# Batch 0's scores and head of softmax in two halves of the tokens, with the mask of the second w_in piece between the halves

**Chip, cores, metric.** One core of one Trainium2 chip. The metric is the device time of one execution in microseconds; the profiled span is about 2 us shorter than that time (750.4 against 752.25 in the profiled run of before). Most comparisons below are of one to four microseconds in 753, so each is backed twice: by timed runs in rounds with the kernel before on the same chip, and by the moment at which one landmark, the first up-projection matmul, starts in the profile.

## The reference

Cross-attention of tokens x (8 batches, 8 heads, 512 tokens, 64 wide) with a small state (32 rows), in both directions, then a two-layer feed-forward with a quick GELU on all 4352 rows.

```python
scores = scale * np.matmul(x, state.transpose(0, 1, 3, 2))
a = softmax(scores);   xread = np.matmul(a, state)      # softmax over the 32 state rows
scores2 = scale * np.matmul(state, x.transpose(0, 1, 3, 2))
a2 = softmax(scores2); sread = np.matmul(a2, x)         # softmax over the 512 tokens
x = concat(xread, sread) reshaped to (B*544, 512)
h = x @ w_in
g = h * (1.0 / (1.0 + np.exp(-1.702 * h)))
out = g @ w_out
```

The weights arrive as float64, so the kernel converts them itself: each of the 16 pieces of w_in is masked (VectorE), turned into a power of two by two Relus (ScalarE), and assembled in four further VectorE instructions ("rounding" below).

## The kernel before

The parts that the change touches, with cuts marked "...".

```python
    def keep_warm(n):                       # fillers: nothing reads the result
        ps = psH.tile([P, FC], FP32, tag="h", name="warm")
        for _ in range(n):
            nc.tensor.matmul(ps, zeros[:, :P], zeros, start=True, stop=True)
    ...
    def round_a(i):
        ...
        nc.vector.tensor_scalar(sc, hi, 0x7FF00000, None, ALU.bitwise_and)          # the mask
        ...
        nc.scalar.activation(out=sc.bitcast(FP32), in_=sc, func=AF.Relu, bias=edge[0], scale=-8.0)
        nc.scalar.activation(out=sc, in_=sc.bitcast(FP32), func=AF.Relu, bias=edge[1], scale=-1.0)
    ...
    def att_xT_arriving(b, warm):
        A[b]["xT"] = apool.tile([P, NPR, S], FP32, tag="xT", name=f"xT_{b}")
        for c in range(SCH):                                                        # 4 chunks of 128 tokens
            keep_warm(warm)
            ps = att_ps([P, NPR, P], f"xT_{b}_{c}")
            for j in range(NPR):
                nc.tensor.transpose(ps[:, j], x_heads(b, c, j), ident)
            (nc.scalar.copy if c % 2 else nc.vector.tensor_copy)(A[b]["xT"][:, :, P * c : P * (c + 1)], ps)
    ...
    load_weights(1); load_state(0); load_x(0); load_weights(NPR); load_state(1); load_x(1); ...   # one per line
    keep_warm(11)
    round_to(1, 0)               # mask, Relus and rounding of piece 0
    att_state(0)
    att_xT_arriving(0, 2)
    att_scores(0)                # 8 matmuls of 512 columns
    powers_to(2)                 # mask and Relus of piece 1
    att_blocks(0)                # VectorE: two transposes of 512 columns
    att_x_exp(0)                 # VectorE: maximum, subtraction; ScalarE: exponential
    round_to(2, 1)
    att_x_norm(0)
    keep_warm(24)
    att_state(1)
    ...                          # batch 1's transposes and scores
    keep_warm(24)
    powers_to(4)
    round_to(NPR, 2)             # pieces 2 and 3
    att_M(0, 0)                  # M(0,0): w_in's first 512 columns times batch 0's state
    att_blocks(1)
    att_x_exp(1)
    up_x(0, 0)                   # first up-projection matmul: the landmark
    ...
```

## Time and profile before

| | before |
|---|---|
| median of three runs, and their spread | 752.65 us, 752.60 to 754.64 |
| profiled span | 750.4 us |
| TensorE busy | 731.6 us, 98% |
| M(0,0) starts | 29.05 us |
| first up-projection matmul starts | 30.89 us |

The page's clock row, one digit for each fortieth of the span (18.8 us), shows the TensorE clock that was granted; a 9 is full speed or nearly. The trace's record of the clock begins with its first change, at 6.06 us; ahead of it the view shows 1.00, while the eleven fillers of the start took 4.88 us, 0.43 each, twice their later 0.22.

```profile
PEclk9999999999999999999999999999999999999999
```

In a view by stretches, a line holds the stretch in us, its length, the busy time of TensorE, its weight loads, VectorE, ScalarE and GpSimd, the granted clock, and the transfers. In the kernel before two stretches are:

```profile
12.00:18.00 6.00, 6.00 (x43) 2.65 (x28) 5.39 (x9) 2.99 (x4) 0.00 (x0) 1.00 0.99 254
18.00:24.00 6.00, 5.49 (x42) 2.86 (x41) 5.83 (x10) 3.71 (x8) 0.00 (x0) 1.00 1.01 322
```

VectorE is busy for 5.4 and 5.8 of 6 us. Below, M(b,c) is the product of w_in's c-th 512 columns with batch b's state.

### The profile page before, as it was taken

The page shows a single profiled execution, that of the slowest core. Times are in us where ns is not written, and L with a number is a line of the kernel's source. Part 1 is how long each engine was busy: PE and PEld are TensorE (multiplying, and loading weights), DVE is VectorE, ACT ScalarE, POOL GpSimd, SP SyncE. Part 2 cuts the span into 40 slices and gives each one's busy share as a digit, 9 for nine tenths or more (in the row PEclk, how much of TensorE's full clock was granted, in tenths as well). Part 3 has the DMA queues.
Part 4 walks back from the last instruction along what each step waited for, and adds up shares of the span by engine and source line. Part 5 has one row for each costly group of instructions (what it writes and reads, how often), then busy time and mean ns, then how long its engine had stood idle before and what let it go on. Part 6 is the DMA issues. An engine that isn't in the chain of part 4 may idle for free.

```text
span 750.4 us, 10915 instructions
## 1 busy us (share of the span) xinstructions
PE 731.6 (98%) x4555; PEld 567.4 (76%) x4555; DVE 501.7 (67%) x947; ACT 232.1 (31%) x421; POOL 0.8 (0%) x8
## 2 busy tenths in 40 slices
PE   8989999999999999999999999999999999999996
PEld 3433444467888789878888789878887888899995
DVE  5999799615846775567747666677656774768340
ACT  4676511022324511433134322451143313300220
POOL 0000000000000000000000000000000000000000
PEclk9999999999999999999999999999999999999999
DMA  9811245010030000300040003000030001000000
GB/s 236 331 58 56 93 160 144 0 57 1 29 83 5 1 16 29 74 1 15 2 102 1 15 2 93 10 1 16 29 74 1 15 2 42 1 15 29 15 1 28
DMA packets 48768, 35.29 MB, mean 47 GB/s; under 512 B 36432, under 2 KB 44112, under 8 KB 48720
## 3 DMA queue, kind: packets, MB, share of 16 engines
q1 hardware_dynamic: 48720, 34.61, 16.1%
q8 instruction: 35, 0.57, 0.3%
q14 instruction: 13, 0.11, 0.1%
HBM read 25.69 MB, written 8.91 MB: 46 GB/s over the span
## 4 chain that ended last, share of the span: by engine, by line
PE 94%; SPq 2%; ACT 2%; DMA 1%; DVE 1%; issue 0%; DVEq 0%; ACTq 0%
PE o L645 28%; PE o L890 16%; PE o L522 9%; PE h L461 8%; PE o L479 7%; PE low L597 6%; PE upx L890 6%; PE o L597 4%; PE M L279 4%; PE xT L261 1%; SPq L138 1%; PE sr L410 1%; PE o L279 1%; PE upx_sr L890 1%; DMA out_dram<-osb_sr 1%; PE warm L122 1%
## 5 line engine op out<-in xcount | busy, mean ns | idle before, releaser
L900 DVE TENSOR_TENSOR g<-o,g 128x512 f32<-128x512 f32 (+1 forms) x140 | 88.1, 651 | 87.3 <-PE o L890 86.3
L645 PE MATMUL o<-w_out,g 128*128 128x256 f32 x576 | 130.0, 380 | 0.0
L645 PEld LDWEIGHTS o<-w_out,g 128*128 128x128 f32 x576 | 107.4, 190 | 18.1 <-issue 4.2
L897 ACT ACTIVATE g<-g 128x512 f32<-128x512 f32 (+1 forms) x84 | 49.8, 600 | 100.5 <-DVE g L900 100.5
L890 PE MATMUL o<-ta,M 128*128 128x256 f32 x192 | 49.3, 379 | 0.0
L890 PE MATMUL upx<-aT,M 128*128 128x256 f32 x192 | 49.3, 379 | 0.0
L890 PE MATMUL o<-ta,ms 128*128 128x256 f32 x192 | 48.4, 380 | 0.0
L390 ACT COPY M<-M 128x512 f32<-128x512 f32 x64 | 33.2, 596 | 42.5 <-PE M L279 42.5
L645 PE MATMUL o<-sums,g 128*128 128x256 f32 x192 | 43.8, 382 | 0.0
L522 PE MATMUL o<-w_out,g 128*128 128x256 f32 x192 | 42.9, 380 | 0.0
L645 PE MATMUL o<-sums,later 128*128 128x256 f32 x192 | 42.4, 379 | 0.0
L645 PEld LDWEIGHTS o<-sums,g 128*128 128x128 f32 x192 | 35.6, 190 | 8.6 <-issue 4.2
L522 PEld LDWEIGHTS o<-w_out,g 128*128 128x128 f32 x192 | 36.1, 190 | 6.0 <-issue 1.3
L890 PEld LDWEIGHTS o<-ta,ms 128*128 128x128 f32 x192 | 36.4, 190 | 5.2 <-DVE osb L541 0.3
L890 PEld LDWEIGHTS o<-ta,M 128*128 128x128 f32 x192 | 36.5, 190 | 5.0
L645 PEld LDWEIGHTS o<-sums,later 128*128 128x128 f32 x192 | 36.5, 190 | 5.0
L890 PEld LDWEIGHTS upx<-aT,M 128*128 128x128 f32 x192 | 36.5, 190 | 5.0
L502 DVE TENSOR_TENSOR later<-g,g 128x512 f32<-128x512 f32 (+1 forms) x32 | 20.8, 650 | 21.5 <-ACT g L464 21.5
L279 PE MATMUL M<-w_in,stT 64*32 64x512 f32 x512 | 33.2, 594 | 0.2 <-ACT eT L400 0.2
L461 PE MATMUL h<-low,M 128*128 128x512 f32 x64 | 29.8, 600 | 2.1 <-ACT M L390 2.1
L461 PE MATMUL h<-aT,M 128*128 128x512 f32 x64 | 28.7, 599 | 2.3 <-ACT M L390 2.3
L600 DVE TENSOR_TENSOR pu<-low,pu 128x128 f32<-128x128 f32 x12 | 3.5, 291 | 39.6 <-PE low L597 39.6
(172 smaller groups left out, 1136.6 us busy)
## 6 DMA issues: line engine op xcount, KB each, us to landing
later<-in_moe_w_out_dram SPq DMA_DIRECT2D x16, 512.0 KB
xn<-in_x_dram SPq DMA_DIRECT2D x28, 256.0 KB
w_out<-in_moe_w_in_dram SPq DMA_DIRECT2D x12, 512.0 KB
out_dram<-osb SPq DMA_DIRECT2D x20, 256.0 KB
out_dram<-later SPq DMA_DIRECT2D x12, 256.0 KB
later<-in_moe_w_in_dram SPq DMA_DIRECT2D x4, 512.0 KB
sums<-in_x_dram SPq DMA_DIRECT2D x4, 256.0 KB
stn<-in_state_dram SPq DMA_DIRECT2D x16, 32.0 KB
```

The lines of the kernel that those rows point to most:

```text
L122: nc.tensor.matmul(ps, zeros[:, :P], zeros, start=True, stop=True)
L279: nc.tensor.matmul(ps[g][st], A[b]["stT"][rows, st], rhs(rows, j), start=True, stop=True)
L390: nc.scalar.copy(m[:, g], ps[g])
L461: nc.tensor.matmul(hps, lhs[i], rhs[i], start=(i == 0), stop=(i == n - 1))
L479: nc.tensor.matmul(ops, G[key, f // 2][:, f % 2, P * r : P * (r + 1)], w_out[:, f], start=(f == 0), stop=(f == NF - 1))
L502: nc.vector.tensor_tensor(out=s1, in0=a21, in1=a22, op=ALU.add)
L522: nc.tensor.matmul(ps[:, r], lhs[f][:, P * r : P * (r + 1)], rhs[:, f], start=(first and r == 0 and f == 0), stop=(f == HF - 1), skip_grou ...
L597: nc.tensor.matmul(ps, lhs[f], rhs[:, f], start=(f == 0), stop=(f == QF - 1))
L645: nc.tensor.matmul(ps[:, r], lhs[f][:, P * r : P * (r + 1)], rhs[:, f], start=(r == 0 and f == 0), stop=(f == HF - 1), skip_group_check=True,)
L890: nc.tensor.matmul(ps[:, k], lhs[i][:, o : o + P], rhs[i], start=(first and k == 0 and i == 0), stop=(i == n - 1), skip_group_check=True,)
L897: nc.scalar.activation(out=dst, in_=src, func=AF.Gelu_apprx_sigmoid)
L900: nc.vector.tensor_tensor(out=dst, in0=ps, in1=x, op=ALU.add)
```

## The change

The intent: VectorE, which paces the opening, waits until all four chunks of batch 0's x have been transposed. If it begins after two of them, its work on the first half lies in time that it had spent waiting. The mask of piece 1 goes between the halves, where VectorE would wait again. As M(0,0) is expected earlier, ten fillers go.

```diff
         for c in range(SCH):
-            keep_warm(warm)
+            if c < 2:
+                keep_warm(warm)
             ps = att_ps([P, NPR, P], f"xT_{b}_{c}")
             ...
-            (nc.scalar.copy if c % 2 else nc.vector.tensor_copy)(A[b]["xT"][:, :, P * c : P * (c + 1)], ps)
+            (nc.scalar.copy if c else nc.vector.tensor_copy)(A[b]["xT"][:, :, P * c : P * (c + 1)], ps)
+            if c % 2:
+                att_half(b, c // 2)
+            if c == 1:
+                powers_to(2)
...
+    def att_half(b, i):
+        ...
+        by_state(b, ps, lambda rows, j: a["xT"][rows, j, n * i : n * (i + 1)])     # 8 matmuls of 256 columns
+        for g in range(NG):
+            nc.vector.transpose(a["e1"][:, g, w].rearrange("p i n -> p (i n)"), ps[g])
+        t, mx = a["e1"][:, :, w], a["mx"][:, :, w]
+        nc.vector.reduce_max(out=mx, in_=t, axis=AX.X)
+        nc.vector.tensor_tensor(out=t, in0=t, in1=mx.to_broadcast((P, NG, NB // 2, Ns)), op=ALU.subtract)
...
     att_xT_arriving(0, 2)
+    nc.scalar.activation(out=A[0]["e1"], in_=A[0]["e1"], func=AF.Exp, scale=scale)
     att_scores(0)
     powers_to(2)
-    att_blocks(0)
-    att_x_exp(0)
...
     att_scores(1)
-    keep_warm(24)
+    keep_warm(14)
     powers_to(4)
```

More of the change, by code (lines that the diff above doesn't have):

```diff
@@ L279, in by_state @@
                 nc.tensor.matmul(ps[g][st], A[b]["stT"][rows, st], rhs(rows, j), start=True, stop=True)
+    def att_half(b, i):
+        a = A[b]
+        if i == 0:
+            a["e1"] = apool.tile([P, NG, NB, Ns], FP32, tag="e1", name=f"e1_{b}")
+            a["mx"] = apool.tile([P, NG, NB], FP32, tag="mx", name=f"mx_{b}")
+        n, w = S // 2, slice(NB // 2 * i, NB // 2 * (i + 1))
+        ps = [v[:, :n] for v in bank_o[NG:]] if i else [psH.tile([P, n], FP32, tag="h", name=f"sh_{b}_{g}") for g in range(NG)]
+        by_state(b, ps, lambda rows, j: a["xT"][rows, j, n * i : n * (i + 1)])
[4 more added lines that the diff above has]
+        nc.vector.tensor_tensor(out=t, in0=t, in1=mx.to_broadcast((P, NG, NB // 2, Ns)), op=ALU.subtract)
     def att_scores(b):
```

## The prediction

> **What bounds the kernel now.** I read the page first. The first line of its busy times, and its chain that ended last (PE 94%), say that nearly the whole span is TensorE work, and the change removes none of that: it touches only the opening, some 30 us of 750.

> ```profile
> PE 731.6 (98%) x4555; PEld 567.4 (76%) x4555; DVE 501.7 (67%) x947; ACT 232.1 (31%) x421; POOL 0.8 (0%) x8
> ```

> So the question is when steady TensorE work starts. The chain of work over the first 60 us (start us, duration us, what) answers:

> ```profile
> 15.03 4.10 DMA sums<-in_x_dram
> ...
> 22.10 1.73 PE o L279 x16
> 23.83 5.29 PE warm L122 x24
> 29.11 1.16 PE M L279 x16
> ...
> 30.89 7.15 PE h L461 x16
> ```

> The chain runs through the arrival of batch 1's x, then batch 1's scores, then 24 filler matmuls (L122 only keeps the array busy), then M(0,0), the product of w_in with batch 0's state at 29.1. A chain through filler needs a second reading: filler is there to fill, so something else may end at the same moment. The timeline of the opening shows it (start us, duration us, engine, line, operation, in brackets idle time and releaser):

> ```profile
> 1.19 4.88 PE L122 MATMUL warm<-sums 128*128 128x512 bf16 x11 [1.19 <-DVE one L113]
> 8.46 0.59 ACT L272 COPY xT<-xT 128x512 f32<-128x512 f32 x1 [1.58 <-PE xT L271]
> 8.70 0.69 DVE L272 COPY xT<-xT 128x512 f32<-128x512 f32 x1
> 10.77 0.59 ACT L272 COPY xT<-xT 128x512 f32<-128x512 f32 x1 [1.72 <-PE xT L271]
> 11.41 1.09 PE L279 MATMUL o<-xT,stT 64*32 64x512 f32 x16 [0.67 <-ACT xT L272]
> 11.63 0.43 DVE L189 TENSOR_SCALAR low<-w_out 128x512 int32<-128x512 int32 x1 [1.14 <-DMA w_out<-in_moe_w_in_dram]
> 12.09 0.72 ACT L194 ACTIVATE low<-low,edge 128x512 f32<-128x512 int32 x1 [0.73 <-DVE low L189]
> 12.44 5.35 PE L122 MATMUL warm<-sums 128*128 128x512 bf16 x24
> 12.59 1.31 DVE L292 STREAM_TRANSPOSE e<-o 128x512 f32<-128x512 f32 x2 [0.54 <-PE o L279]
> 13.94 1.22 DVE L328 TENSOR_REDUCE mx<-e 128x32 f32<-128x1024 f32 x1
> 15.20 1.22 DVE L329 TENSOR_TENSOR e<-e,mx 128x1024 f32<-128x1024 f32 x1
> 16.34 0.42 DVE L189 TENSOR_SCALAR low<-w_out 128x512 int32<-128x512 int32 x1
> ...
> 28.12 0.69 DVE L207 SCALAR_TENSOR_TENSOR w_in<-w_in,low 128x512 f32<-128x512 f32 x1
> ...
> 29.05 1.09 PE L279 MATMUL M<-w_in,stT 64*32 64x512 f32 x16
> ```

> From 12.59 to 28.81 (28.12 + 0.69) VectorE has no wait: head of batch 0's softmax, then rounding of w_in pieces, with piece 3 last. M(0,0) needs piece 3 and starts 0.24 later. Hence **VectorE is the real bound of the opening**, and the 24 fillers are sized to end with it. The time from the end of the subtraction (15.20 + 1.22 = 16.42) to piece 3 is 12.39 us of unchanged VectorE work. After M(0,0) the chain is matmuls, evictions and short Relus, and TensorE is almost without gaps from 49 us on, so a shift of M(0,0) should reach the end whole.

> [...] ScalarE's instructions up to 31 us stand in program order. [...] 11 fillers in 4.88 us (0.43 each) at the start, against 24 in 5.35 (0.22) later[...]. [...] a reduction over 1024 elements takes 1.22 us and one over 512 (L299, later) 0.68, so two halves cost 0.14 more.

> **The change part by part.** *Removed:* two pairs of fillers in front of the third and fourth chunk of x; VectorE's copy of chunk 2 (0.69, now a ScalarE copy of 0.59); ten of the later fillers (10 x 0.22 = 2.2 us of TensorE). *Added:* two half-width score products on TensorE (the full one stays, because the second softmax reads it). Their matmuls are half as long, so about 0.5 us each in the queue and about 0.65 to the first result (1.09 less half of 0.86, the latter being the spacing of 16 such matmuls in row "PE M L279 x32", 1.72 us). On VectorE, per half: two transposes of 256 columns. With (1.22 - 0.68)/512 = 1.05 ns per column, 0.72 becomes 0.45 and the pair 0.77 us; a reduction over 512, 0.68; a subtraction over 512, about 0.69; two gaps of 0.04: 2.22 us. Two halves are 4.44 against 3.83 (12.59 to 16.42), so 0.6 more VectorE work, to be repaid by starting earlier.

> *Moved:* the mask of piece 1 (L189) with its two ScalarE Relus (L194, L195), from behind the scores to between the halves. This is the step on which I decide. My timetable:
> - VectorE copies chunk 0 to 9.39 as now. Half-scores 0 on TensorE 9.44 to 10.1. VectorE half 0 from 10.2 to 12.45. Its mask of piece 1 about 12.4 to 12.8 (the data has been there since 11.63).
> - TensorE transposes chunks 2 and 3 by about 11.1. Their copies are both on ScalarE, and in its program they stand **behind the two Relus of piece 1**, which wait for the mask, which waits for half 0. Relus from 12.85 to 14.3, copy of chunk 2 to 14.85, of chunk 3 to 15.4.
> - Half-scores 1 at 15.45, first result 16.2; VectorE, idle since 12.8 (some 3.4 us), does half 1 from 16.3 to 18.5.
> - 18.5 against 16.42 is 2.1 us later. The 12.39 us of unchanged work then end at 30.9 and M(0,0) starts at 31.1 in place of 29.05.

> TensorE on its side: full scores about 16.0 to 17.0, 24 fillers to 22.35, stT and the four transposes of batch 1 (3.9 us without today's wait of 0.5 for x, which arrived at 19.1) to 26.1, scores to 27.8, 14 fillers (14 x 0.22 = 3.1) to 30.9. That agrees with VectorE's 31.1, so the cut from 24 to 14 neither costs nor helps. Relus of piece 3 come behind batch 1's copies, at about 26.8 to 28.3, just before VectorE wants them at 28.9.

> The sum: M(0,0) **2.1 us later**, so 752.65 + 2.1 = 754.75.

> **The rivals.** *1. The intended gain.* If the copies of chunks 2 and 3 were not held behind the Relus, they would end near 11.85, half-scores 1 would be ready at 12.6, and VectorE would go on from the mask (12.8) to 15.05: 1.4 us earlier than 16.42. TensorE, held by x at 19.17 as now, would have scores to 23.8 and fillers to 26.9, under VectorE's 27.4. Total 751.2. For it: the cut of ten fillers (2.2 us) looks like someone expecting an earlier M(0,0). Against it: the order of calls and ScalarE's order in the trace. I give it 1 in 8.

> *2. A cold array.* The removed fillers leave TensorE without work from about 11.1 to 15.45, 4.4 us [...]. [...] Then half-scores, scores and many of the 24 fillers run at half rate for some 4 us (4.3 us at the start of this trace), which costs about 2 us: TensorE reaches M(0,0) at about 33 and becomes the bound in place of VectorE. Total 752.65 + 4.0, about 756.6. I give it 0.4.

> *3. A delay hidden behind transfers.* Batch 1's x arrives at 19.1 and pins TensorE today. It would hide a small TensorE delay (about 0.5 us), but not VectorE's chain, which doesn't wait for it, and weights arrive ahead of VectorE. So little is hidden; I give a zero change 1 in 10.

> **Range and chances.** With 0.45 on +2.1, 0.4 on about +4, and the rest at or below zero, the middle is near +2.6: 755.2. The runs before spread by 2 us (752.6 to 754.64), so the range is 752.6 to 757.4. Two per cent is 15 us; no rival comes near that, so "within 2%" gets 0.985.

> **What would show each step.** Right: ScalarE's two Relus of piece 1 near 12.9, ahead of the copies of chunks 2 and 3, whose idle time is put down to PE or to DVE's mask; an idle VectorE for about 3.4 us ahead of the second pair of 256-column transposes near 16.3; M(0,0) near 31. Clock: 24 fillers in 5.35 us means a warm array, 7 us or more a cold one. Wrong: copies of chunks 2 and 3 near 10.7 and 11.3 ahead of the Relus (then rival 1); a half's VectorE work much over 2.2 us; or a later VectorE wait or a gap in TensorE between 31 and 160 us that grows or shrinks, so that the shift at M(0,0) is not the shift of the end.

The sum has all its terms: 752.65 + 2.1 = 754.75. The point of 755.2 comes from 752.65 + 0.45 x 2.1 + 0.4 x 4.0, and the 0.4, the chance of rival 2, stands as the author's estimate. The length of half rate in rival 2, some 4 us, is an estimate from the fillers at the start of the trace: 0.43 us each, so that ten are 4.3.

## The result, and the profile after

The changed kernel has a median of 756.91 us (four runs, 756.16 to 757.40), and the kernel before, in the same rounds, 753.25 (752.60 to 754.64). The ratio is 1.0045, with a 95% interval of 1.0027 to 1.0064: slower by about 3.4 us, within 2%. A ratio here is the mean time of one kernel's fast runs over that of the other's in the same rounds, so it is not quite the ratio of the medians.

The timeline of the changed kernel, as in the prediction: start us, duration us, engine, line, operation, and in brackets the idle time before it with what ended it. Its lines are those that answer to the ones shown of before.

```profile
8.91 0.68 DVE L273 COPY xT<-xT 128x512 f32<-128x512 f32 x1
9.74 0.67 PE L284 MATMUL sh<-xT,stT 64*32 64x256 f32 x16 [1.19 <-DVE xT L273]
10.34 1.09 PE L272 MATMUL xT<-ident,xn 128*128 128x128 f32 x8
10.48 0.78 DVE L296 STREAM_TRANSPOSE e<-sh 128x256 f32<-128x256 f32 x2 [0.89 <-PE sh L284]
12.02 0.69 DVE L299 TENSOR_TENSOR e<-e,mx 128x512 f32<-128x512 f32 x1
12.63 0.42 DVE L189 TENSOR_SCALAR low<-w_out 128x512 int32<-128x512 int32 x1
13.09 0.72 ACT L194 ACTIVATE low<-low,edge 128x512 f32<-128x512 int32 x1 [3.91 <-DVE low L189]
13.84 0.72 ACT L195 ACTIVATE low<-low,edge 128x512 int32<-128x512 f32 x1
14.47 1.05 ACT L273 COPY xT<-xT 128x512 f32<-128x512 f32 x2
15.57 2.81 PE L284 MATMUL o<-xT,stT 64*32 64x256 f32 x32 [4.14 <-ACT xT L273]
16.77 0.78 DVE L296 STREAM_TRANSPOSE e<-o 128x256 f32<-128x256 f32 x2 [3.72 <-PE o L284]
18.30 0.69 DVE L299 TENSOR_TENSOR e<-e,mx 128x512 f32<-128x512 f32 x1
19.15 6.04 PE L122 MATMUL warm<-sums 128*128 128x512 bf16 x22 [0.22 <-issue]
...
30.80 0.69 DVE L205 SCALAR_TENSOR_TENSOR low<-w_out,low 128x512 int32<-128x512 int32 x1 [1.33 <-ACT low L195]
33.55 1.09 PE L284 MATMUL M<-w_in,stT 64*32 64x512 f32 x16
35.40 7.13 PE L481 MATMUL h<-aT,M 128*128 128x512 f32 x16 [0.76 <-ACT M L410]
```

The transposes of chunks 2 and 3 are done at 11.43, but the copies start at 14.47: ScalarE has the two Relus of piece 1 ahead of them, and sat idle for 3.91 us until VectorE's mask let those go. VectorE in turn was idle for 3.72 us until the second half's scores came. Its subtraction ends at 18.99 in place of 16.42.

The second thing is the length of TensorE's work after its gap of 4.14 us. The view by stretches has the same 12 us as above:

```profile
12.00:18.00 6.00, 2.43 (x32) 0.67 (x32) 2.23 (x5) 2.40 (x4) 0.00 (x0) 0.72 1.06 262
18.00:24.00 6.00, 5.78 (x27) 2.33 (x21) 5.83 (x11) 2.39 (x3) 0.00 (x0) 0.71 1.00 355
```

The granted clock is 0.72 and 0.71. The kept trace lists every change of the clock: it falls from 1.00 to 0.50 at 14.59 us and is back at 1.00 at 21.42. That is half rate for 6.83 us, during which the second half's scores and the full scores took 2.81 us in all and a filler 0.43. The mean clock is 0.993 in each of the four runs, against 0.998 in the profiled run of before, so every run of the changed kernel seems to have lost about as much.

Does the shift reach the end whole? The chain that ended last, at one piece of work near 185 us and one near 585, first before, then after:

```profile
185.24 10.56 PE o L522 x48
583.23 10.56 PE o L645 x48
```

```profile
189.76 10.34 PE o L542 x47
587.76 10.56 PE o L665 x48
```

The shift is 4.52 and 4.53 us; at the first up-projection matmul it was 35.40 - 30.89 = 4.51. TensorE's last matmul ends 4.53 us later too, so nothing is absorbed or added on TensorE after the opening; the spans differ by 4.8, the last 0.3 after TensorE has ended. The medians differ by less (3.7 us), probably because some runs of the kernel before lose time at another place, which the experiments found.

### The profile page after: what moved, and what is told of

It is laid out like the page before. It is cut to its first block, busy times and chain, and to the rows that moved or that the text cites. A ratio compares the mean times of both kernels' runs of the same rounds, so it can differ in the third digit from the quotient of the medians.

```text
span 755.2 us, 10952 instructions
## 1 busy us (share of the span) xinstructions
PE 731.3 (97%) x4571; PEld 566.9 (75%) x4573; DVE 501.7 (66%) x950; ACT 232.3 (31%) x422; POOL 0.8 (0%) x8
## 3 DMA queue, kind: packets, MB, share of 16 engines
HBM read 25.69 MB, written 8.91 MB: 46 GB/s over the span
## 4 chain that ended last, share of the span: by engine, by line
PE 94%; ACT 2%; DMA 1%; DVE 1%; issue 0%; DVEq 0%; ACTq 0%
PE o L665 28%; PE o L910 16%; PE o L542 9%; PE h L481 8%; PE o L499 7%; PE low L617 6%; PE upx L910 5%; PE o L617 4%; PE M L284 4%; PE warm L122 2%; PE xT L261 1%; PE o L284 1%; PE sr L430 1%; PE upx_sr L910 1%; DMA out_dram<-osb_sr 1%; PE eT L419 1%
## 5 line engine op out<-in xcount | busy, mean ns | idle before, releaser
L481 PE MATMUL h<-low,M 128*128 128x512 f32 x64 | 29.8, 600 | 2.1 <-ACT M L410 2.1
```

Of the source, the lines that this page charges most:

```text
L481: nc.tensor.matmul(hps, lhs[i], rhs[i], start=(i == 0), stop=(i == n - 1))
```

## The experiments

The theory: (a) ScalarE's queue held the copies of chunks 2 and 3 behind the Relus of piece 1, which delayed VectorE; (b) the hole that this left in TensorE's work sent the array to half rate, which made TensorE later still and the bound in place of VectorE. Rivals: the halves themselves are too dear for VectorE; half rate is a bystander; a transfer is the cause. The last can be answered from the changed kernel's own profile: from 8.5 to 36 us no engine has a wait that is put down to a transfer. Eight kernels ran, all correct, on two chips: e1, e2, e3 and e6 on one, e8, e9, e7 and e4 on the other. The kernel before ran with each: 753.6 (752.34 to 755.07) in the first, 754.3 (752.42 to 754.82) in the second, eleven runs each.

| kernel | median us (range of fast runs) | ratio to before (95%) | first up-projection, us |
|---|---|---|---|
| before (profiled run 752.25) | see above | 1 | 30.89 |
| changed | 756.91 (756.16 to 757.40) | 1.0045 (1.0027 to 1.0064) | 35.40 |
| e1: Relus behind the copies | 752.37 (750.94 to 752.83) | 0.998 (0.9967 to 0.9993) | see text |
| e2: gap filled | 755.81 (754.14 to 755.92) | 1.0023 (1.001 to 1.0037) | 32.75 |
| e3: mask late | 754.22 (752.67 to 754.46) | 1.0005 (0.9992 to 1.0018) | 31.19 |
| e6: 14 first fillers | 756.16 (755.62 to 756.55) | 1.0034 (1.0022 to 1.0046) | 32.92 |
| e8: before, filled | 752.75 (752.45 to 753.41) | 0.9986 (0.9971 to 1.0001) | 32.17 |
| e9: both gaps filled | 754.17 (753.96 to 754.26) | 1.0004 (0.9991 to 1.0017) | 32.43 |
| e7: e1, filled | 751.04 (750.71 to 751.72) | 0.9964 (0.9951 to 0.9978) | 29.47 |
| e4: before, 14 fillers | 753.62 (751.92 to 753.92) | 0.9991 (0.9977 to 1.0006) | 30.63 |

### e1: the Relus of piece 1 behind the copies

```diff
             (nc.scalar.copy if c else nc.vector.tensor_copy)(...)
+            if c == SCH - 1:
+                relus(1)                      # the two ScalarE Relus alone
             if c % 2:
                 att_half(b, c // 2)
             if c == 1:
-                powers_to(2)
+                load_weights(2)
+                round_a(1, wait=True)         # the VectorE mask alone
+                done["a"] = 2
```

> The changed kernel with one order altered: VectorE's mask of piece 1 stays between the halves, but ScalarE's two Relus of that piece are issued behind the copies of chunks 2 and 3. Theory (ScalarE's in-order queue held the copies, the idle TensorE then went cold): the copies run near 10.9 and 11.5 us, half-scores 1 near 12.2, VectorE goes from the mask (to 13.05) straight into half 1 and ends it near 15.3, the granted clock of the opening stays at 1.00, M(0,0) starts near 27.9 (after: 33.55, before: 29.05), and the time is about 1.2 us below before. Rival (two halves are dearer for VectorE than thought, or the idle stretch comes from a late transfer): half 1 ends no earlier than 16.4 and M(0,0) is at 29 or later, time at or above before.

The profiled run was throttled as a whole (mean clock 0.829, 878.96 us) and is left out of the times; why, no run tells. The five others have a median of 752.37, 1.2 below before, as expected, though this mixes two groups of runs (see e8). The profile of the same opening at full clock came with e7. VectorE and then ScalarE there:

```profile
10.29 0.78 DVE L305 STREAM_TRANSPOSE e<-sh 128x256 f32<-128x256 f32 x2 [0.89 <-PE sh L293]
...
12.44 0.42 DVE L189 TENSOR_SCALAR low<-w_out 128x512 int32<-128x512 int32 x1
12.77 0.77 DVE L305 STREAM_TRANSPOSE e<-o 128x256 f32<-128x256 f32 x2
...
14.30 0.69 DVE L308 TENSOR_TENSOR e<-e,mx 128x512 f32<-128x512 f32 x1
```

```profile
10.84 1.07 ACT L278 COPY xT<-xT 128x512 f32<-128x512 f32 x2 [1.70 <-PE xT L277]
12.89 0.72 ACT L199 ACTIVATE low<-low,edge 128x512 f32<-128x512 int32 x1 [0.98 <-DVE low L189]
```

The copies run at 10.84, ahead of the Relus, and the second half's transposes follow the mask with no wait in brackets. The head of softmax ends at 14.99, against 16.42 before and 18.99 in the changed kernel. So the halves are not too dear, and part (a) is shown: two instructions in another place of ScalarE's queue turn the loss into a gain. As the gap closes with them, this alone does not part (a) from (b); e2 and e9 do.

### e2: fillers in the gap

```diff
             (nc.scalar.copy if c else nc.vector.tensor_copy)(...)
+            if c == SCH - 1:
+                keep_warm(18)
```

> The changed kernel with 18 fillers (3.9 us) behind the transposes of chunk 3, so that TensorE is busy while ScalarE's Relus hold the copies. Theory (two terms: the held copies cost about 2.2 us, the cold array about 2.3 on top): granted clock 1.00 all through, the 24 fillers 5.35 us, VectorE the bound again with the end of its subtraction near 18.6, M(0,0) near 31.3, time about 2.2 us below the changed kernel, that is about 2 above before. Rival (half rate is a bystander, VectorE alone sets M(0,0)): clock 1.00 but M(0,0) stays within 0.7 us of 33.55.

The landmark is 2.65 us earlier than in the changed kernel (32.75 against 35.40), with nothing altered but useless work. The rival, that half rate is a bystander, falls. The time, though, fell by only 1.1 us in the median (1.7 by the two ratios), against 2.2 expected, and the six runs form two groups: two at 754.14 and 754.15, four at 755.74 to 755.92. The profile is of the upper group and shows why, in the chain and in the stretches from 43 us on:

```profile
43.78 8.76 PE h L483 x16
```

```profile
43.00:44.00 1.00, 0.23 (x1) 0.23 (x2) 0.97 (x3) 1.00 (x3) 0.00 (x0) 0.82 0.00 0
44.00:45.00 1.00, 1.00 (x2) 0.48 (x3) 0.96 (x3) 0.21 (x1) 0.00 (x0) 0.50 0.00 0
45.00:46.00 1.00, 1.00 (x2) 0.46 (x2) 1.00 (x3) 0.00 (x0) 0.00 (x0) 0.50 0.04 8
46.00:48.00 2.00, 2.00 (x4) 0.71 (x3) 1.93 (x5) 0.59 (x2) 0.00 (x0) 0.74 0.00 0
```

Sixteen matmul records of the up-projection took 8.8 us, where the profile of before has 7.15. This is a second spell of half rate, 1.6 us dear, behind M(1,0), where TensorE waits 2.12 us in this kernel as in the one before. That raised a new question: is the spread of the kernel before the same spell? Of its 22 runs, 8 lie below 753, 10 at 754.19 or above, and 4 between.

### e3: the halves alone, mask and Relus as late as before

```diff
-            if c == 1:
-                powers_to(2)
```

> The changed kernel with the mask and Relus of piece 1 behind both halves and the scores, as in the kernel before: the halves alone. Theory: nothing holds the copies (near 10.9 and 11.5 us), half 1 ends near 15.1, no cold array; but the Relus of piece 1 now stand behind the exponential on ScalarE and end near 17.7, and the rounding of piece 1 waits for them, so M(0,0) is near 29.8, about 0.7 later than before; time within 1 us of before. Rival (the halves themselves cause the delay): M(0,0) at 31 or later.

The copies run at 10.98, half 1 ends at 15.09, and the clock of the opening is 1.00. What was won is lost again: the rounding of piece 1 waited for the late Relus, and the last four matmuls of M(0,0), which alone need piece 3, waited for VectorE (the twelve before them had started at 27.41).

```profile
17.58 0.69 DVE L205 SCALAR_TENSOR_TENSOR low<-w_out,low 128x512 int32<-128x512 int32 x1 [1.48 <-ACT low L195]
...
29.47 1.05 PE L282 MATMUL M<-w_in,stT 64*32 64x512 f32 x4 [0.99 <-DVE w_in L207]
```

So putting the mask between the halves was sound, for VectorE. It was the Relus, which came along with it, that were in the wrong place. The landmark is 0.3 later than before, the time the same within the noise.

### e6: 14 instead of 24 fillers behind the scores of batch 0

```diff
     att_x_norm(0)
-    keep_warm(24)
+    keep_warm(14)
```

> The changed kernel with 14 in place of 24 fillers behind the scores of batch 0. Theory (in the changed kernel TensorE's queue, lengthened by the half rate, sets M(0,0), and through batch 1's copies it also delays the Relus of piece 3): the array still goes cold, TensorE is 2.1 us earlier, VectorE's wait of 1.33 us for the Relus of piece 3 goes, M(0,0) near 31.6, time about 1.9 us below the changed kernel. Rival (VectorE's delay alone sets it): M(0,0) stays at 32.8 or later.

Here the array still goes cold (clock 0.60 from 12 to 18 us), but TensorE's queue is shorter. VectorE's wait of 1.33 us is gone and the landmark is at 32.92, 2.5 earlier than in the changed kernel: half rate cost time mostly through TensorE's queue, as in (b). About 0.5 us came another way: the second half's first scores reached VectorE 1.20 us after TensorE had begun them, against 0.75 in e9. The median fell by 0.75 alone, a miss against the expected 1.9. The profile has the second spell again (8.81 us for the sixteen records against 7.15), which gives back 1.66. Whether all five runs have it is not shown: their mean clocks go from 0.991 to 0.995, and the times do not follow them.

### e8: the kernel before with its own gap filled

```diff
     att_x_norm(1)
     att_M(1, 0)
+    keep_warm(9)
```

> The kernel before with 9 fillers (1.94 us) behind M(1,0), where TensorE waits 2.1 us for ScalarE's copies. Theory (the 2 us spread of the kernel before comes from a spell of half rate near 43 us that begins in some executions only, 8.8 instead of 7.15 us for 16 matmuls): no spell any more, every run within 0.8 us of the lowest run of before (about 752.4), median about 1 us below that of before. Rival (the spread comes from transfers or elsewhere): runs stay spread over 2 us, median unchanged or 0.2 higher.

All five runs lie between 752.45 and 753.41; of the eleven runs of the kernel before on the same chip, seven lie at 754.29 or above. The median fell by 1.5 us, and the ratio's interval just reaches 1. One run, 753.41, misses the expected 0.8 us from 752.4. I take the upper group of the kernel before to be the spell near 43 us: the distance fits, filling the gap removes it, and the variant e4 below, whose profile shows the spell, has the same two groups. No profiled run of the unaltered kernel before shows it, but the mean clock is 0.995 to 0.997 in all ten runs at 754.19 or above, 0.998 or more in all twelve below. A spell of 3.41 us at half rate (e3 has it from 43.40 to 46.82) takes 0.0023 off the mean over 751 us, which is that distance. The profile of e8 is of its slowest run and has another, smaller cause of spread: batch 1's x landed at 20.4 instead of 19.1, and the landmark was 32.17. With 24 fillers behind it, so late an x moves the landmark by as much.

### e9: the changed kernel with both gaps filled

The edits of e2 and e8 together.

> The changed kernel with both gaps filled (18 fillers while ScalarE holds the copies, 9 behind M(1,0)): the cost of the held copies with no half rate anywhere. Theory: granted clock 1.00 to 60 us, first up-projection matmul near 32.8 us (e2: 32.75, before: 30.89), so 1.9 us above e8, near 754.2, with little spread. Rival (half rate had no part in the change's cost): no faster than the changed kernel's 756.9.

```profile
12.00:18.00 6.00, 5.74 (x53) 2.28 (x51) 2.65 (x6) 2.40 (x4) 0.00 (x0) 1.00 1.03 271
18.00:24.00 6.00, 6.00 (x34) 3.33 (x32) 5.83 (x11) 3.26 (x6) 0.00 (x0) 1.00 1.00 320
```

The clock is whole, VectorE is still idle for more than half of the first stretch, and the runs are within 0.3 us of each other. This splits the loss. By the landmark: held copies 32.43 - 30.89 = 1.5 us, half rate 35.40 - 32.43 = 3.0, together the 4.5 of the changed kernel. Counted from VectorE's copy of chunk 0 (8.70 before, 8.91 changed, 8.63 here), it is 1.6 and 2.7. By the medians: held copies 754.17 - 752.75 = 1.4 (against e8), half rate 756.91 - 754.17 = 2.7 (another chip, so less sure).

### e7: the first experiment with the gap filled

The edits of e1 and e8 together.

> The first experiment (Relus behind the copies) with 9 fillers behind M(1,0); its opening also replaces the profile that fell in a throttled run. Theory: half 1 ends near 15.3 us on VectorE, VectorE is the bound, M(0,0) near 27.9, first up-projection matmul near 29.6 (before: 30.89), granted clock 1.00, no spread over 1 us, time near 751.2, that is about 1.2 us below e8. Rival (x of batch 1, landing at 19.1, or the Relus of piece 3 hold VectorE or TensorE, so that the halves gain nothing): first up-projection matmul at 30.5 or later, time at that of e8.

```profile
27.14 1.66 PE L293 MATMUL M<-w_in,stT 64*32 64x512 f32 x16
29.47 0.70 PE L490 MATMUL h<-aT,M 128*128 128x512 f32 x1 [0.67 <-ACT M L419]
```

The landmark is 1.4 us earlier than before, the clock 1.00 throughout. The median is 751.04, 1.7 below e8 and 0.36% below before. From e8 it differs by the whole change with the Relus in the right place, so the cut of ten fillers is in it too; alone (e4) that cut moved the landmark by 0.3. This version beats both kernels, and its slowest run is faster than the fastest of before.

### e4: the kernel before with 14 fillers

```diff
     att_scores(1)
-    keep_warm(24)
+    keep_warm(14)
```

> The kernel before with 14 in place of 24 fillers behind the scores of batch 1. Theory (VectorE's rounding of piece 3 sets M(0,0), the filler is no part of the bound): TensorE idles about 2.1 us, M(0,0) starts at 29.0 as before and the first up-projection matmul at 30.9; time as before within 0.5 us, unless that gap of 2.1 us itself brings a spell of half rate in some runs (then 1.7 us more in those). Rival (the chain through the fillers, as the page shows it, is the bound): M(0,0) near 27, time 2 us less.

The chain of waits now goes through VectorE where it went through fillers, and the landmark stays within 0.3 us of before (30.63). The first line below is from the timeline, the others from the chain:

```profile
27.45 1.08 PE L279 MATMUL M<-w_in,stT 64*32 64x512 f32 x12
...
28.16 0.70 DVE w_in L207
...
28.91 1.10 PE M L279 x4
...
41.65 8.85 PE h L461 x16
```

So the second reading of the chain was right: VectorE's rounding of piece 3 is the bound. But only the last four of M(0,0)'s sixteen matmuls need that piece; the other twelve started at 27.45, where the expectation had put all of it at 29.0. It is the landmark, not the start of M(0,0), that decides. The last line is the spell of half rate, in the profiled run of a kernel that has the old opening; its runs fall into two groups, two near 752.0 and four at 753.6 to 753.9.

## Why the prediction was right, and where it was not

- **Bound of the opening: right.** e4 takes ten fillers away and the landmark stays within 0.3 us, as do the four matmuls of M(0,0) that need piece 3. The shift of the landmark reached TensorE's end whole (4.51, 4.52, 4.53 us). "Almost without gaps from 49 us on" leaves out one of 1.51 us, before 51.57; the changed kernel has the same, so it absorbed nothing.
- **Held copies: right in kind and in place.** The Relus of piece 1 ran at 13.09, ahead of the copies at 14.47, where 12.85 and 14.3 had been put down. VectorE idled 3.72 us for a predicted 3.4. The term was set at 2.1 us; with the clock kept whole it measured 1.4 to 1.6. VectorE itself ended piece 3 by 1.85 us later in e9 (30.66 against 28.81). The rest fits the cut from 24 to 14 fillers, which the prediction took to be worth nothing and which brought 0.3 alone (e4): M(0,0) started 0.24 us after VectorE's end before, and 0.19 ahead of it in e9.
- **Rival 1, the intended gain: rejected for this kernel, and its number right for the right order.** An end of the first head of softmax 1.4 us earlier was worked out for copies that nothing holds; e7 has 16.42 - 14.99 = 1.43.
- **Rival 2, the cold array: under-weighted and mis-sized.** It got a chance of 0.4 and about 2 us more. All four runs have the clock of the cold opening, and it cost 2.7 to 3.0 us. The term that failed is the length of half rate: about 4 us had been taken from the fillers at the start of the trace, and it was 6.83. The chance of 0.4 was the author's estimate; all four runs went cold, and in e6 1.99 us of idle time in one stretch was followed by half rate (below). Scores took 2.81 us where e2 has 1.52, and the 24 fillers 6.9 us (18.32 to 25.19) where 5.35 is normal: 2.8 us together. The point of 755.2 was a mean over the rivals (whose chances, 0.4, 1 in 8 and 1 in 10, add up with the 0.45 of its own timetable to more than one). The measured 756.91 lies in the range, which held all rivals but the first, and is almost that of rival 2 (756.6). That nearness is in part luck: its 4.0 us against a measured 4.5 at the landmark came from one term too large and one too small, and the median of before had moved up by 0.6.
- **Rival 3, a delay hidden behind x: no.** The landmark moved by the whole delay.
- **Relus of piece 3 "just before VectorE wants them": wrong once the array is cold.** They stand behind batch 1's copies, which came later with TensorE, and VectorE waited 1.33 us.
- **Half rate in some executions of the kernel before: missed.** Its profile shows none between 6.06 us and the end of TensorE, but a gap of 2.12 us behind M(1,0), which it has too, was followed by half rate in the profiles of e2, e3, e4 and e6. What the prediction took for noise of 2 us is mostly that spell, so far as e8, e4 and the clocks of the runs show it.

| profile | stretch, us | TensorE idle in it, us | clock after it |
|---|---|---|---|
| changed, opening | 11.18 to 14.59 | 3.16 | 0.50 |
| e6, opening | 9.77 to 13.18 | 1.99 | 0.50 |
| e2, behind M(1,0) | 40.23 to 43.64 | 1.98 | 0.50 |
| e3, behind M(1,0) | 39.99 to 43.40 | 2.12 | 0.50 |
| e4, behind M(1,0) | 38.63 to 42.05 | 2.12 | 0.50 |
| e6, behind M(1,0) | 40.49 to 43.90 | 2.07 | 0.50 |
| before, behind M(1,0) | 40.19 to 43.61 | 1.72 | 1.00 |
| changed, behind M(1,0) | 41.90 to 45.31, 45.31 to 48.73 | 1.00, 1.12 | 1.00 |

No other full-rate stretch before TensorE's last matmul has more than 1.51 us. So the same gap of 2.12 us falls into one stretch in some executions and is split between two in others. A gap of 4.14 us leaves at least 2.07 in one stretch wherever it falls, which fits the cold opening in all four runs of the changed kernel (mean clock 0.993). This is read from nine profiles and was not tested by an experiment; nor was it tested whether half rate sets in at one value between 1.72 and 1.98 us, or whether the kind of work around the gap matters.

The way back was read in the same stretches. The spell behind M(1,0) in e3 lasted one of them (43.40 to 46.82 us), the one in the opening of the changed kernel two: after 2.44 us of TensorE work in the first (14.59 to 18.01) the clock stayed at 0.50, after 3.19 in the second (18.01 to 21.42) it was 1.00, as it was after 3.17 us at the kernel's start (0.94 to 4.35, where the fillers took 0.43 us each).

## What to carry to other kernels

When a piece of work is moved, all its instructions move, on every engine: look in each engine's program at what now stands behind them and whom they wait for (here two copies behind two Relus that waited for a mask, 1.4 to 1.6 us). Filler that looks useless can pay where TensorE would wait (here 2.12 us in e8, with 1.5 us off the median, and 4.14 in e2 and e9, with 2.65 off the landmark in e2), and a chain that runs through filler does not tell the bound: take some out and see whether the next real instruction moves. Times that fall into two groups are a finding, not noise; look for the group's mark in the profile and in the mean clock of each run before averaging over it.
